# Second router's logits at three places of each feature tile, and the next item's rows transposed inside an earlier product

## The chip, the cores and the metric

The kernel runs on one core of a Trainium2 chip. The metric is the device time of one execution in microseconds (us). The engines are TensorE (PE in the rows; PEld is its loading of weights), VectorE (DVE), ScalarE (ACT), GpSimd (POOL) and SyncE (SP), which issues most transfers.

## The reference

One launch computes an attention layer, a mixture of experts with two experts per token, and a second mixture with one expert per token. The second router can only run on tokens whose first mixture is complete.

```python
def _moe_ref(x, w_gate, w_noise, noise, w1, w2):            # first layer, top 2 of E = 8 experts
    ...
    for e in range(E):
        for k in range(2):
            mask = top2[:, k] == e
            h = np.maximum(x[mask] @ w1[e], 0.0)
            out[mask] += top2_w[mask, k, None] * (h @ w2[e])

def _moe2_ref(x, modality_id, w_gate, modality_bias, w1, w2):   # second layer, one expert per token
    logits = x @ w_gate + modality_bias[modality_id]
    e_idx = np.argmax(logits, axis=1)
    logits_s = logits - logits.max(-1, keepdims=True)
    probs = np.exp(logits_s)
    probs /= probs.sum(-1, keepdims=True) + 1e-09
    gate_w = probs[np.arange(N), e_idx]
    ...
    for e in range(E):
        mask = e_idx == e
        h = np.maximum(x[mask] @ w1[e], 0.0)
        out[mask] = gate_w[mask, None] * (h @ w2[e])

def reference(**kwargs):
    ...
    attn_out = _attn_ref(**attn_kwargs)                     # 4 x 8 heads x 576 x 64
    x = np.ascontiguousarray(attn_out.transpose(0, 2, 1, 3)).reshape(B * S, H * D)
    x = _moe_ref(x=x, **moe_kwargs)                         # N = 2304 tokens, D = 512, F = 1024
    return _moe2_ref(x=x, **moe2_kwargs)
```


## The kernel before

The matrix products of both mixtures are a list of 20 **items**, numbered from 0, each being one expert with a block of gathered token rows. Items 0 to 3 (256 rows) and 4 to 7 (384 rows) are experts 0 to 3 of the first mixture in two parts, items 8 to 11 (640 rows) its experts 4 to 7. Items 12 to 19 belong to the second mixture: item 12 has 512 rows of the expert that the router finds to be the commonest, items 13 and 14 have 256. In the code `L7` is 11, the last item of the first mixture, so `L7 + 1` is item 12.

An item runs over eight **feature tiles**, f = 0 to 7, of 128 hidden features. In the order of issue, f of an item is: loading weights (`_load`) and splitting the weights of two tiles on into a high and a low part (`_split`: `whi` on ScalarE, `wlo` on VectorE or GpSimd); `_first(s + 1)`, which is layer 1 of the next tile (L727, 24 products of 320 columns for 640 rows) with its eviction from PSUM to `hh` (ScalarE, L729) and `hl` (VectorE, L730); then layer 2 of tile f (L739, three products of 512 columns for each block of 128 rows). Item 11 has five such blocks, so 15 products; after the second block `mid()` is called. All engines work through their instructions in the order in which the program issues them.

The `hook` is called three times in each f: with half 0 after layer 1 and ahead of layer 2, with half 2 in `mid()`, and with half 1 after layer 2. The text calls these places **half 0**, **mid** and **end**. In items 11 to 13 the hook runs the second router. `token_tiles` takes two blocks of 128 finished tokens at a place: `px` (L1323) transposes them, at the next place `pl` (L1328) forms their logits, and at the one after `plT` (L1335) transposes the logits back for VectorE (L1337, L1340). There are 18 blocks, so nine places with `px`. Their rows are loaded by SyncE into `x2l`, four blocks at first and two more as two are used up. All these PSUM tiles, and those of layer 1, share one tag, `h`, with three buffers.

Beside this, `back` is a queue of generators that `tick` advances, up to 24 steps per place in item 11. `piece(k)` routes a range of tokens: tops of the logits, then `places` on TensorE (L485 to L488), then the one-hot pairs `ol`, `oh` on VectorE (L526, L527) and `invert` on TensorE (L532). A generator that yields "PE" stops until a later place, and `unblock` lets it go. `choose` finds the commonest expert, `first(item, ...)` finds the rows of item 12: it counts tokens on TensorE (L1380), works out the indices on VectorE (`chd`, L1408, to `pi`, L647), and issues the gather of `xg` on GpSimd (L701). `DONE` names the places at which `need` drives the queue until such a step has been issued.

`_transpose` turns gathered rows into `xh` and `xl`, which layer 1 reads: products `pt` (L710) on TensorE, then ScalarE (L712) and VectorE (L713). For item 12 `tight=1` puts it in f = 7 of item 11, ahead of layer 2, and moves layer 1 of item 12 behind that layer 2.

These few lines of `run` and `second_router` decide the places:

```python
            if nxt and f == nxt.get("at", 0) and i + 1 not in self.rows:
                self._gather(i + 1)
            ...
                n = nxt.get("per", 2)
                j = n * (f - nxt.get("from", FB - 4))
                if nxt and not nxt.get("tight") and j >= 0 and f < FB - 1:
                    self._transpose(i + 1, j, j + n)
```

Of the kernel before, what the change touches and what calls it, by code (L numbers as in the profile page):

```python
# [534 lines left out]
class Items:  # L535
# [87 lines left out]
    def next(self):  # L623

        nc, w, tag, nt = self.nc, self.consts, self.tag, self.nt
        m = w.tile([128, self.most], F32, tag=f"{tag}nm", name="nm")
        j = w.tile([128, self.most], F32, tag=f"{tag}nj", name="nj")
        r = w.tile([128, 1 + nt], F32, tag=f"{tag}nr", name="nr")
        ei = w.tile([128, 1], I32, tag=f"{tag}nei", name="nei")
        nc.vector.tensor_scalar(m, self.ij, self.count, None, op0=ALU.is_equal)  # L630
        for a, src in enumerate([self.ei] + [self.col[:, a] for a in range(nt)]):
            nc.vector.tensor_tensor(j, m, src, op=ALU.mult)
            nc.vector.tensor_reduce(r[:, a:a + 1], j, axis=AX.X, op=ALU.add)
        nc.vector.tensor_copy(ei, r[:, 0:1])
        nc.vector.tensor_scalar(self.count, self.count, 1.0, None, op0=ALU.add)
        return dict(e=ei[0:1], e128=r[:, 0:1], col=[r[:, 1 + a:2 + a] for a in range(nt)])
# [216 lines left out]
def core(ctx, tc, q, k, v, moe_w_gate, moe_w_noise, moe_noise, moe_w1, moe_w2,  # L853
# [37 lines left out]
    ffn = FFN(nc, wpool, DM, F, identF)  # L891
# [4 lines left out]
    with ExitStack() as actx:  # L896
# [135 lines left out]
        back, wait, age = [], [False], [0]  # L1032

        def tick(n=1, pe=False):

            if pe:
                wait[0] = False
            while n and back and not wait[0]:
                n -= 1
                try:  # L1040
                    what = next(back[0])
                    wait[0] = what in ("PE", "PE soon") and not pe
                    age[0] = 2 if what == "PE soon" else 0
                except StopIteration:
                    back.pop(0)

        def unblock(lag=0):

            if wait[0]:
                if age[0] < lag:  # L1050
                    age[0] += 1
                else:
                    wait[0] = False
                    tick(1)
# [147 lines left out]
    def cols(e, j0=0, j1=5):  # L1202
        return [idx[:, e * NT + j:e * NT + j + 1] for j in range(j0, j1)]
# [92 lines left out]
    top = consts.tile([128, 1, E], F32, tag="top", name="top")  # L1296
    tope = consts.tile([128, 1], F32, tag="tope", name="tope")
    topi = consts.tile([128, 1], I32, tag="topi", name="topi")
# [5 lines left out]
    L7 = NX + LAST  # L1304
# [71 lines left out]
    def counts():  # L1376

        yield "PE soon"
        pc = bank2()
        nc.tensor.matmul(pc[:, :E], rt.ones, base2, start=True, stop=True)  # L1380
        yield
        return pc[:, None, :E]

    def need(what):
        while what not in done:
            tick(1, True)

    def choose():

        V = nc.vector  # L1390
        pc = yield from counts()
        cnt, w = (route.tile([128, 1, E], F32, tag=f"ch{n}", name=f"ch{n}") for n in "cw")
        V.tensor_copy(cnt, pc)
        yield
        yield from rt.top(cnt, 1, [top])
        V.tensor_tensor(w, top, rt.iE[:, None], op=ALU.mult)
        yield
        V.tensor_reduce(tope, w, axis=AX.XY, op=ALU.add)
        yield
        V.tensor_copy(topi, tope)  # L1400
        done.add("top")

    def first(item, c0, c1):

        V = nc.vector
        pc = yield from counts()
        d = route.tile([128, 1, E], F32, tag="chd", name="chd")
        V.tensor_scalar(d, pc, -1.0, 128.0 * c1, op0=ALU.mult, op1=ALU.add)  # L1408
        V.scalar_tensor_tensor(topc, tope.to_broadcast([128, 6]), float(NT), rt.iE[:, :6], op0=ALU.mult, op1=ALU.add)
        yield  # L1410
        V.tensor_scalar(d, d, rt.p128, 0.0, op0=ALU.subtract, op1=ALU.max)
        yield
        V.scalar_tensor_tensor(d, d, 128.0, top, op0=ALU.min, op1=ALU.mult)
        yield
        V.tensor_tensor(base2[:, None], base2[:, None], d, op=ALU.add)
        yield from decode2()
        ix = it2.pick(fpool, [topc[:, a:a + 1] for a in range(c0, c1)], ft)
        ffn.items[item].update(rows=lambda: ffn.gather(x2_rows[:, :], ix), out=out2(ix), e=lambda: expert(topi[0:1]),
                               w1=moe2_w1, w2=moe2_w2, ns=128 * (c1 - c0), banks=range(c1 - c0))
        ffn._gather(item)  # L1420
        done.add(item)

    def decode2():
        yield from rt.decode(fs, tab, rt.padh)
        nc.vector.tensor_scalar(ft, fs, rt.pad, None, op0=ALU.subtract)
        yield

    def cut2():
        pc = yield from counts()
        yield from odd_one(pc[:, 0])  # L1430
        yield from it2.cut(pc[:, 0], taken, STATIC)
        done.add("cut")
# [40 lines left out]
    def gates_of(c0, c1):  # L1473
        def write():
            nc.sync.dma_start(x2_rows[128 * c0:128 * c1, DM:DM + 1].rearrange("(t p) c -> p t c", p=128),
                              gate[:, c0:c1, None])
        return write
# [15 lines left out]
    def expert(ap):  # L1493
        return nc.values_load(ap, engines=[mybir.EngineType.SP], min_val=0, max_val=E - 1,
                              skip_runtime_bounds_check_because="experts are counted on the chip")

    def out2(ix):
        def outp(a, p, meta):
            scatter(out, ix[a], weighted(p, meta[:, 0:1])[:, :DM], outs, bounds_check=N - 1, oob_is_err=False)
        return outp  # L1500

    ffn.items[L7 + 1].update(e=lambda: expert(topi[0:1]), at=7, late=True, tight=1)
    ffn.items[L7 + 2].update(e=lambda: expert(topi[0:1]), at=5, **{"from": 5}, pool=True)
    ffn.items[L7 + 3].update(at=1)

# [18 lines left out]
    def load_tiles(n):  # L1524
        for t in loads[:n]:
            x2 = late_pool[0].tile([128, DM], F32, tag="x2l", name="x2l", bufs=4)
            nc.sync.dma_start(x2, x2_rows[128 * t:128 * t + 128, :DM])
            pend.append((t, x2))
        del loads[:n]
# [11 lines left out]
    def token_tiles(n):  # L1541
        new = [(t, x2, wb[:, t, E:]) for t, x2 in pend[:n]]
        del pend[:n]
        tiles(new)
        load_tiles(n)

    def last_tiles(j0, j1):
        tiles([(NT + j, x2, meta[:, E:2 * E]) for j, x2, meta in st2[j0:j1]])

    def piece(k):  # L1550
        c0, c1 = PIECES[k]
        back.append(route2(c0, c1, rt.code[:, c0:c1], gates_of(c0, c1)) if c1 <= NT else
                    route2(c0, c1, code2, gates_last))

    def second_router(i, f, half):

        busy = f == 7 and i == L7
        if half == 0:
            if not busy:
                unblock(1)  # L1560
                tick(TICKS[i - L7])
            return
        h = 2 * (f + 8 * (i - L7)) + half % 2
        if h == 0:
            nc.gpsimd.memset(tab, 0.0)
            fl = fs[:, LAST * NT:LAST * NT + 5]
            rt.encode(code2, fl)
            nc.vector.tensor_scalar(valid[:, NT:], fl, float(N), None, op0=ALU.is_lt)
            nc.vector.tensor_scalar(valid[:, :NT], early, -1.0, 1.0, op0=ALU.mult, op1=ALU.add)
        if h == 1:  # L1570
            load_tiles(4)
        if h == 4:
            rest.extend(ffn.gather(x2_rows[:, :], cols(LAST), tag="rest", bufs=5))
        if h in TILES:
            token_tiles(TILES[h])
        if h in LASTS:
            last_tiles(*LASTS[h])
        if h in WHEN:
            WHEN[h]()
        if not busy:  # L1580
            unblock(1)
            tick(TICKS[i - L7])
        if h in DONE:
            need(DONE[h])

    TICKS = (24, 6, 3)
    DONE = {9: "top", 11: L7 + 1, 25: L7 + 2, 33: "cut"}
    TILES = {**{h: 2 for h in range(2, 11)}, 11: 0, 12: 0}
    LASTS = {17: (0, 2), 18: (2, 4), 19: (4, 5), 20: (5, 5), 21: (5, 5)}

    WHEN = {5: lambda: (piece(0), back.append(choose())), 9: lambda: (piece(1), back.append(first(L7 + 1, 0, 4))),
            12: lambda: (piece(2), back.append(first(L7 + 2, 4, 6))),
            21: lambda: (piece(3), back.append(decode2()), back.append(cut2()))}

    def hook(i, f, half):
        now[0] = i
# [55 lines left out]
```

## Time and profile before

| | us |
|---|---|
| median of 3 runs | 922.13 (921.55 to 924.22) |
| profiled execution | 923.1 |
| its span | 921.4 |
| TensorE busy in the span | 866.3 (94%) |
| VectorE, ScalarE, GpSimd busy | 543.3, 429.3, 322.7 |

The profiled execution is 1.0 us above the median, and 1.7 us of it lie outside its span. A row of a timeline gives the start in us from the span's beginning, the length, engine, line, operation, output and inputs, a count, and in brackets the engine's idle time just before and what ended it. TensorE's products overlap, so a row's length is longer than the step to the next row: a run of products of 512 columns steps by about 0.235 us while each row says 0.39. The clock column is a share of full speed, so 1.00 is 2.4 GHz and 0.50 is 1.2 GHz.

### The profile page before, as it was taken

How to read it: one execution, taken by the hardware profiler on the slowest of the kernel's cores; microseconds unless marked ns; L12 is line 12 of the kernel's file. 1: busy time of each engine (PE TensorE's matmuls, PEld its weight loads, DVE VectorE, ACT ScalarE, POOL GpSimd, SP SyncE). 2: the span in 40 equal slices, each digit the busy share in tenths (PEclk: the TensorE clock that was granted, in tenths of full speed). 3: DMA queues.
4: the chain of work that ended last, by engine and by line, in shares of the span. 5: the costliest groups of instructions: out<-in, count | busy, mean ns of one | idle time of the engine just before them, and what ended most of it. 6: DMA issues, size and time to landing. Idle time of an engine off the chain costs nothing. (4 is left out here: it accounts for less than half of the span.)

```text
span 921.4 us, 18166 instructions
## 1 busy us (share of the span) xinstructions
PE 866.3 (94%) x6775; PEld 760.6 (83%) x6775; DVE 543.3 (59%) x1317; ACT 429.3 (47%) x949; POOL 322.7 (35%) x460
## 2 busy tenths in 40 slices
PE   6998986699999999999999999989989999999995
PEld 5777875598898989999898999978867889999995
DVE  5676796379875544544343443434666877556662
ACT  4575654355554434444233342334423356455662
POOL 7767668235553123043006032050020442222210
PEclk9899998899999999999999999999999999999998
DMA  7868799435886557476328245175423477546660
GB/s 168 179 131 202 175 268 337 151 137 143 275 246 194 147 151 193 142 193 151 126 74 180 92 92 162 46 156 171 129 96 115 149 246 245 186 158 219 209 217 24
DMA packets 158702, 153.83 MB, mean 167 GB/s; under 512 B 74319, under 2 KB 119887, under 8 KB 158608
## 3 DMA queue, kind: packets, MB, share of 16 engines
q1 hardware_dynamic: 143936, 115.43, 41.0%
q0 software_dynamic: 12080, 32.45, 15.2%
q10 hardware_dynamic: 2592, 4.72, 1.4%
q8 instruction: 56, 0.92, 0.4%
q14 instruction: 38, 0.31, 0.1%
HBM read 124.98 MB, written 27.85 MB: 166 GB/s over the span
## 5 line engine op out<-in xcount | busy, mean ns | idle before, releaser
L727 PE MATMUL ph<-xh,whi 128*128 128x256 f32 (+3 forms) x768 | 238.0, 310 | 2.8 <-DVE wlo L688 2.1
L727 PE MATMUL ph<-xl,whi 128*128 128x256 f32 (+3 forms) x768 | 237.1, 309 | 0.4 <-DVE xl L713 0.3
L727 PE MATMUL ph<-xh,wlo 128*128 128x256 f32 (+3 forms) x768 | 237.0, 309 | 0.1
L739 PE MATMUL y<-whi,hh 128*128 128x512 f32 x472 | 191.2, 405 | 0.0
L739 PE MATMUL y<-wlo,hh 128*128 128x512 f32 x472 | 187.2, 397 | 0.0
L688 DVE TENSOR_TENSOR wlo<-raw,whi 128x512 fp32r<-128x512 f32 x135 | 93.3, 691 | 159.2 <-ACT whi L687 147.2
L739 PE MATMUL y<-whi,hl 128*128 128x512 f32 x472 | 186.5, 395 | 0.0
L687 ACT ACTIVATE whi<-raw 128x512 fp32r<-128x512 f32 x160 | 101.0, 631 | 168.4 <-PE y L739 153.8
L727 PEld LDWEIGHTS ph<-xh,whi 128*128 128x128 f32 x768 | 145.6, 190 | 12.7 <-issue 2.6
L727 PEld LDWEIGHTS ph<-xl,whi 128*128 128x128 f32 x768 | 145.6, 190 | 8.3 <-DVE xl L713 1.0
L729 ACT ACTIVATE hh<-ph 128x256 fp32r<-128x256 f32 (+3 forms) x192 | 83.3, 434 | 140.7 <-PE ph L727 133.7
L727 PEld LDWEIGHTS ph<-xh,wlo 128*128 128x128 f32 x768 | 145.8, 190 | 1.8 <-DVE wlo L688 0.3
L730 DVE SCALAR_TENSOR_TENSOR hl<-ph,hh 128x256 fp32r<-128x256 f32 (+3 forms) x192 | 92.5, 482 | 84.1 <-ACT hh L729 81.8
L1196 POOL DMA_INDIRECT x_rows<-y,idx x35 | 57.7, 1648 | 206.6 <-ACT y L1187 106.5
L690 DVE TENSOR_TENSOR wlo<-raw,whi 128x512 fp32r<-128x512 f32 x160 | 119.5, 747 | 12.1 <-ACT whi L689 10.8
L739 PEld LDWEIGHTS y<-whi,hl 128*128 128x128 f32 x472 | 89.0, 188 | 21.2
L739 PEld LDWEIGHTS y<-whi,hh 128*128 128x128 f32 x472 | 89.5, 190 | 13.1 <-DVE y L1189 0.2
L739 PEld LDWEIGHTS y<-wlo,hh 128*128 128x128 f32 x472 | 89.3, 189 | 12.6
L689 ACT ACTIVATE whi<-raw 128x512 fp32r<-128x512 f32 x160 | 98.7, 617 | 0.6 <-DMA raw<-in_moe_w_dram 0.6
L713 DVE TENSOR_TENSOR xl<-pt,xh 128x512 fp32r<-128x512 f32 x59 | 38.8, 688 | 31.0 <-ACT xh L712 30.8
L1196 POOL DMA_INDIRECT out_dram<-y,pi x19 | 20.6, 1084 | 99.6 <-ACT y L1187 44.3
L269 POOL TENSOR_TENSOR Pd<-pe,sm 32x380 f32<-32x380 f32 (+1 forms) x48 | 42.1, 877 | 35.0 <-DVE smd L40 20.0
(302 smaller groups left out, 1076.9 us busy)
## 6 DMA issues: line engine op xcount, KB each, us to landing
raw<-in_moe_w_dram SPq DMA_DIRECT2D x160, 512.0 KB
x_rows<-zero SPq DMA_DIRECT2D x1, 5934.0 KB
vr<-in_v_dram SPq DMA_DIRECT2D x16, 288.0 KB
x_rows<-xr ACTq DMA_DIRECT2D x18, 256.0 KB
x2l<-x_rows SPq DMA_DIRECT2D x18, 256.0 KB
qk<-in_q_dram SPq DMA_DIRECT2D x32, 128.0 KB
qk<-in_k_dram SPq DMA_DIRECT2D x32, 128.0 KB
vw<-in_v_dram SPq DMA_DIRECT2D x24, 128.0 KB
```

What stands on the lines that cost most here:

```text
L269: eng.tensor_tensor(Pd[s, :, W * g:W * g + n], pe[s, :, :n], sm[s, :, None].to_broadcast([W, 2 * NB, n]), op=ALU.mult)
L687: nc.scalar.activation(h1, a, AF.Copy)
L688: eng.tensor_tensor(l1, a, h1.bitcast(F32), op=ALU.subtract)
L689: nc.scalar.activation(hi[:, 1], r2[:, half], AF.Copy)
L690: nc.vector.tensor_tensor(lo[:, 1], r2[:, half], hi[:, 1].bitcast(F32), op=ALU.subtract)
L713: nc.vector.tensor_tensor(xl, p, xh.bitcast(F32), op=ALU.subtract)
L727: nc.tensor.matmul(ps, w[a][:, k], x[b][:, k, s], start=(i == 0), stop=(i == 3 * KD - 1))
L729: nc.scalar.activation(hh[:, s], ps, AF.Relu)
L730: nc.vector.scalar_tensor_tensor(hl[:, s], ps, 0.0, hh[:, s].bitcast(F32), op0=ALU.max, op1=ALU.subtract)
L739: nc.tensor.matmul(p, h[a][:, 128 * j:128 * j + 128], w[b], start=(f == 0 and i == 0), stop=(f == self.FB - 1 and i == 2))
L1196: d = nc.gpsimd.indirect_dma_start(out=dst, out_offset=bass.IndirectOffsetOnAxis(ap=ix, axis=0), in_=y, in_offset=None, **kw)
```

## The change

The hook of item 11 uses half 0 as well as mid and end, so h counts three places for each f there (h = 3f, 3f + 1, 3f + 2) and two for each f from item 12 on (from h = 24). The tables are renumbered. In terms of places: the first `px` moves from f = 1 mid to f = 1 end, and the ninth from f = 5 mid to f = 4 mid; `piece(0)` and `choose` stay at f = 2 end; `piece(1)` and `first` of item 12 move from f = 4 end to f = 4 half 0; the place at which `first` of item 12 must have been issued moves from f = 5 end to f = 6 half 0; `piece(2)` moves from f = 6 mid to f = 6 half 0. Item 12 loses `tight=1` and gets `per=4, from=6`: its four blocks are transposed in f = 6 mid, and its layer 1 is issued ahead of layer 2 of f = 7.

```diff
-    ffn.items[L7 + 1].update(e=lambda: expert(topi[0:1]), at=7, late=True, tight=1)
+    ffn.items[L7 + 1].update(e=lambda: expert(topi[0:1]), at=7, late=True, per=4, **{"from": 6})
...
-        if half == 0:
-            if not busy:
-                unblock(1)
-                tick(TICKS[i - L7])
+        late = i > L7
+        if late and half == 0:
+            unblock(1)
+            tick(TICKS[i - L7])
             return
-        h = 2 * (f + 8 * (i - L7)) + half % 2
+
+        h = 24 + 2 * (f + 8 * (i - L7 - 1)) + half % 2 if late else 3 * f + (0, 2, 1)[half]
...
-        if h == 1:
+        if h == 2:
             load_tiles(4)
...
-    DONE = {9: "top", 11: L7 + 1, 25: L7 + 2, 33: "cut"}
-    TILES = {**{h: 2 for h in range(2, 11)}, 11: 0, 12: 0}
-    LASTS = {17: (0, 2), 18: (2, 4), 19: (4, 5), 20: (5, 5), 21: (5, 5)}
+    DONE = {14: "top", 18: L7 + 1, 33: L7 + 2, 41: "cut"}
+    TILES = {**{h: 2 for h in range(5, 14)}, 14: 0, 15: 0}
+    LASTS = {25: (0, 2), 26: (2, 4), 27: (4, 5), 28: (5, 5), 29: (5, 5)}
...
-    WHEN = {5: lambda: (piece(0), back.append(choose())), 9: lambda: (piece(1), back.append(first(L7 + 1, 0, 4))),
-            12: lambda: (piece(2), back.append(first(L7 + 2, 4, 6))),
-            21: lambda: (piece(3), back.append(decode2()), back.append(cut2()))}
+    WHEN = {8: lambda: (piece(0), back.append(choose())), 12: lambda: (piece(1), back.append(first(L7 + 1, 0, 4))),
+            18: lambda: (piece(2), back.append(first(L7 + 2, 4, 6))),
+            29: lambda: (piece(3), back.append(decode2()), back.append(cut2()))}
```

On TensorE, in f = 5 and 6 of item 11, the count for `first` (L1380) stands in the kernel before behind the last `invert` of f = 5 and ahead of layer 1.

```order
L532 LDWEIGHTS ol
L532 MATMUL rbank<-oh,ol 128x144
L1380 LDWEIGHTS r_ones
L1380 MATMUL rbank<-base_3095,r_ones 128x8
L727 MATMUL ph<-xh,whi 128x320
L727 MATMUL ph<-xl,whi 128x320
```

Behind these rows stand the rest of layer 1's 24 products, six of layer 2 (`y_7576`, `y_7577`), one `plT`, nine more of layer 2, and then the 16 transposes of item 12 (L710). In the changed kernel the count stands behind layer 1, and the transposes follow six products later:

```order
L727 MATMUL ph<-xh,wlo 128x320
L1380 LDWEIGHTS r_ones
L1380 MATMUL rbank<-base_3095,r_ones 128x8
L739 MATMUL y_7576<-whi,hh 128x512
L739 MATMUL y_7576<-wlo,hh 128x512
L739 MATMUL y_7576<-whi,hl 128x512
L739 MATMUL y_7577<-whi,hh 128x512
L739 MATMUL y_7577<-wlo,hh 128x512
L739 MATMUL y_7577<-whi,hl 128x512
L710 MATMUL pt<-gw,xg 128x128 x16
L739 MATMUL y_7578<-whi,hh 128x512
```

So between count and transposes there were 39 products of the item and there are now 6.

On VectorE the same stretch, as a piece of the difference from the last one-hot pair of `piece(1)` to the first instruction behind the count (`chd`):

```order
 L527 TENSOR_SCALAR oh<-r_hHI,lchi,r_code 128x144
-L1337 TENSOR_REDUCE l_3097<-plT 128x16
-L1340 TENSOR_TENSOR l_3097<-l_3097,wb 128x8 x2
 L1373 TENSOR_TENSOR tab<-tab,rbank 128x144
+L688 TENSOR_TENSOR wlo<-raw,whi 128x512
+L690 TENSOR_TENSOR wlo<-raw,whi 128x512
+L730 SCALAR_TENSOR_TENSOR hl<-ph,hh 128x320 x2
 L1408 TENSOR_SCALAR chd<-rbank 128x8
```

The split of a weight tile and both evictions of layer 1 now stand ahead of `chd`, where they stood behind the whole index computation.

On GpSimd the gathers of items 12 and 13 stand in the kernel before as

```order
L701 DMA rest<-x_rows,idx 128x516 x5
L701 DMA xg<-x_rows,pi 128x516 x4
L786 COPY meta<-xg 128x4 x4
L701 DMA xg<-x_rows,pi 128x516 x2
```

and in the changed kernel as

```order
L701 DMA rest<-x_rows,idx 128x516 x5
L701 DMA xg<-x_rows,pi 128x516 x4
L786 COPY meta<-xg 128x4 x4
L701 DMA xg<-x_rows,pi 128x516 x6
```

Four gathers have been added: `_transpose` has dropped item 12's rows at f = 6, so the test of `run` at f = 7 (`at=7`) finds none and gathers the same rows a second time; nothing reads them.

## Rows read from the trace of the kernel before

**Rows 1.** Windows of 20 us: length, then busy PE, PEld, DVE, ACT, POOL; clock, DMA, GB/s.

```profile
620.00:640.00 20.00, 20.00 (x149) 16.22 (x148) 7.67 (x31) 9.22 (x21) 0.60 (x1) 1.00 0.58 201
...
660.00:680.00 20.00, 16.57 (x109) 13.04 (x110) 15.98 (x71) 6.91 (x15) 5.11 (x8) 0.95 0.55 159
```

**Rows 2.** TensorE's own waits from 690 us to the end, one row in all.

```profile
PE pt L710 <- DMA xg<-x_rows,pi: 0.4, 1, 0.4
```

**Rows 3.** Timeline of TensorE in item 11, f = 1 and 2.

```profile
617.02 1.39 PE L1323 MATMUL px<-gw,x2l 128*128 128x128 f32 x8 [2.53 <-DMA x2l<-x_rows]
...
625.62 0.39 PE L739 MATMUL y<-whi,hh 128*128 128x512 f32 x1
...
627.02 0.38 PE L1335 MATMUL plT<-gw,lT 128*128 128x128 f32 x2
627.33 0.64 PE L1328 MATMUL pl<-x2T,g 128*32 128x256 f32 x8
627.90 1.09 PE L1323 MATMUL px<-gw,x2l 128*128 128x128 f32 x8
```

**Rows 4.** Timeline of TensorE in item 11, end of f = 5 to f = 7.

```profile
664.70 0.81 PE L532 MATMUL rbank<-oh,ol 128*128 128x144 f16 x6
665.68 0.22 PE L532 MATMUL rbank<-oh,ol 128*128 128x144 f16 x1 [0.17 <-DVE oh L527]
665.74 0.17 PE L1380 MATMUL rbank<-base,r_ones 128*128 128x8 bf16 x1
...
669.45 0.39 PE L739 MATMUL y<-whi,hh 128*128 128x512 f32 x1
...
672.94 0.40 PE L739 MATMUL y<-whi,hl 128*128 128x512 f32 x1
674.89 0.63 PE L710 MATMUL pt<-gw,xg 128*128 128x128 f32 x4 [1.55 <-DMA xg<-x_rows,pi]
...
677.75 2.04 PE L710 MATMUL pt<-gw,xg 128*128 128x128 f32 x8 [0.80 <-DMA xg<-x_rows,pi]
679.44 0.78 PE L739 MATMUL y<-whi,hh 128*128 128x512 f32 x1
```

**Rows 5.** Timeline of VectorE in item 11.

```profile
626.28 0.49 DVE L730 SCALAR_TENSOR_TENSOR hl<-ph,hh 128x320 fp32r<-128x320 f32 x1 [1.12 <-ACT hh L729]
...
660.03 0.23 DVE L1337 TENSOR_REDUCE l<-plT 128x16 f32<-128x64 f32 x1 [0.66 <-PE plT L1335]
...
661.68 0.17 DVE L498 TENSOR_TENSOR base<-base,more 128x8 bf16<-128x8 bf16 x1 [0.66 <-PE rbank L486]
...
665.30 0.32 DVE L527 TENSOR_SCALAR oh<-r_hHI,lchi,r_code 128x144 f16<-128x144 f16 x1
...
666.16 0.16 DVE L1408 TENSOR_SCALAR chd<-rbank 128x8 f32<-128x8 f32 x1
...
670.06 0.23 DVE L647 TENSOR_SCALAR pi<-ps,r_pad 128x4 int32<-128x4 f32 x1
```

**Rows 6.** Timeline of GpSimd from the gathers of item 12 on.

```profile
671.03 1.27 POOL L701 DMA_INDIRECT xg<-x_rows,pi  x1 [50.43 <-DVE wlo L688]
...
675.12 0.95 POOL L701 DMA_INDIRECT xg<-x_rows,pi  x1 [0.30 <-issue]
...
678.61 0.19 POOL L786 COPY meta<-xg 128x4 f32<-128x4 f32 x1 [0.76 <-DMA xg<-x_rows,pi]
708.94 0.98 POOL L701 DMA_INDIRECT xg<-x_rows,pi  x1 [30.14 <-DVE l L1340]
```

**Rows 7.** Timeline of TensorE at its longest wait, early in the program.

```profile
176.94 1.97 PE L710 MATMUL pt<-gw,xg 128*128 128x128 f32 x8 [5.71 <-DVE lg L969]
```

**Rows 8.** Busy time in windows of 1 us at two places, columns as in rows 1.

```profile
176.00:177.00 1.00, 0.06 (x1) 0.06 (x1) 0.23 (x1) 0.60 (x1) 0.81 (x1) 0.52 0.60 148
...
186.00:187.00 1.00, 1.00 (x6) 0.77 (x5) 0.56 (x2) 0.28 (x2) 0.00 (x0) 0.86 0.00 0
...
681.00:682.00 1.00, 1.00 (x6) 0.80 (x5) 0.94 (x3) 0.00 (x0) 0.00 (x0) 0.89 0.00 0
```

## The prediction

> **What bounds the kernel now.** I read the busy time in windows first. From 620 to 640 us TensorE is busy in 20.00 of 20 us at full clock; from 660 to 680, where item 11 ends, in 16.57, with the clock at 0.95 [rows 1]. Then I asked for TensorE's waits behind that: from 690 us to the end they sum to 0.4 us [rows 2]. So TensorE sets the end from item 11 on, and whatever its queue gains or loses in item 11 arrives at the end unchanged. The timelines of the engines in item 11 then show two places where it stands still. One is the first `px` at f = 1 mid: 2.53 us until the rows `x2l` land [rows 3]. The other is the tight transposition in f = 7: the last product of layer 2 of f = 6 starts at 672.94, layer 2 of f = 7 starts at 679.44, and between them stand 16 transposes with waits of 1.55, some 0.8 and 0.80 us for the gathered rows [rows 4].
>
> **First part: `px` one place later.** The wait ends at 617.02 and began 2.53 earlier, at 614.49 [rows 3]. In the changed kernel the nine products of layer 2 of f = 1 that are left come first. Fifteen such products and a small `plT` run from 669.45 to 673.17 in [rows 4] (672.94 plus a step of 0.23); `plT` costs 0.22 of this with the step back, so fifteen cost 3.5 and nine 2.1. TensorE then asks at 616.6 for rows that land at 617.0: a wait of 0.4 stays, **-2.1 us**. Bounds: -1.5, if the landing that ended the wait was the first block's and the second comes later still, and -2.5, the whole wait.
>
> **Half 0 costs a PSUM wait.** Layer 1 and the router's tiles share three buffers. At half 0, `plT`, `pl` and `px` follow right behind layer 1. The last `hl` that empties a buffer of layer 1 ends at 626.77, 1.15 us after the product that follows layer 1 started [rows 3, 5]; `plT` and `pl` fill only 0.88 of that (627.02 to 627.90 [rows 3]), or 0.57 at f = 2, where there is no `plT`. At mid, six products (1.4 us) cover this wait. There are three such places (f = 2, 3 and 4). Nothing in this trace has the wait, so I bound each from 0 (another buffer is free) to 0.6, and take 0.2, nearer to the 0.3 that the two rows leave than to the upper end: **+0.6 us**, bounds 0 and 1.8.
>
> **`places` of `piece(1)` at f = 5 half 0.** Before, it stood at mid and VectorE was ready ahead of TensorE. Now VectorE must first finish `hl` (to 1.1 us after layer 1). From the logits' reduction at 660.03 to the update of `base` at 661.68 less its wait of 0.66 are 0.99 us, and from there to the end of the last one-hot pair (665.62) 3.94 [rows 5]: in sum 6.0 us after layer 1. TensorE fills `plT` (0.31 [rows 3]), `places` (eight small products, by estimate 0.2, since they overlap as the seven `invert` products do), 15 products (3.5) and seven `invert` products, of which six take from 664.70 to 665.68, less the wait of 0.17, so 0.81, and seven 0.95 [rows 4]: in sum 5.0. It waits about 1.1 where it waited 0.17: **+0.9 us**, bounds 0 and 1.3.
>
> **The transposes at f = 6 mid.** This is the large term. Count from the first product of layer 2 of f = 6. Before, it starts at 669.45, and layer 2 of f = 7 at 679.44: 9.99 us with all of f = 6 and the transposes in them [rows 4]. The count (L1380) stood at 665.74, ahead of layer 1, and covered 3.7 us more of the chain. In the changed kernel the count comes behind layer 1, and `chd` on VectorE behind `hl`, which ends 1.15 after layer 1; with the overlap of one instruction into the next, `chd` starts at 1.1. From `chd` (666.16) to the end of `pi` (670.29) are 4.13 [rows 5]. GpSimd starts the first gather 0.74 later (671.03 [rows 6]). From there to the first product behind the transposes are 8.41 (679.44 [rows 4, 6]). Layer 2 of f = 6 thus resumes 1.1 + 4.13 + 0.74 + 8.41 = 14.4 us after it began, with only six products (1.4) and the transposes done in that time. Nine products more, 2.1, make 16.5 against 9.99, and the `plT` that was inside the 9.99 is paid elsewhere (0.22): **+6.7 us**, bounds 5.9 (`chd` right behind the count) and 7.2 (half a microsecond more in four landings that could vary). No other engine hides any of it: TensorE's own work was the cover, 39 products before and 6 now, and a product behind a waiting one cannot pass it.
>
> Behind the transposes the 2.1 us of layer 2 and `places` still cover `xh` and `xl` of the last block, one instruction each on ScalarE and VectorE, so layer 1 of item 12 need not wait; without that cover it would wait the length of those two. Moving layer 1 of item 12 ahead of layer 2 of f = 7 costs nothing in itself: the same products in another order.
>
> One rule of the Trainium skill bears on the gathers. The last gather's issue ends at 676.07 and its rows are there at 678.61, 2.54 later; the first one's ends at 672.30 and the transposes start at 674.89, 2.59 later [rows 4, 6]. "DMA: Bandwidth & Descriptors", section "Latency and other measured facts", puts the access time of the memory at 0.2 us on average and 2 us under high load, so that a lighter load shortens a transfer's fixed part. By that page the quieter traffic at the new place would give an estimated 1.8 us back, and the sum would be 4.9. By the rows, first and last gather take the same, and I keep 8.41.
>
> **The clock.** After TensorE stood still for 5.71 us until 176.94 [rows 7], the granted clock fell to half (0.52 in the window from 176) and came back within the window from 186, 0.86, that is at 186.3 [rows 8]: 9.3 us after the first transposes. In item 11 now, it came back in the window from 681, 0.89, at 681.2, so 1.8 us of layer 2 ran at half and lost 0.9. In the changed kernel the engine stands idle for 8.4 us ahead of the transposes, so they run at half clock; the first three still wait for landings and lose nothing. If the return takes as long as at 176, it comes 9.3 after the first transposes, 4.7 after resuming, and loses 2.4, 1.5 more than now; if it takes as long as at 674.89 to 681.2, 6.3, it loses no more than now. I take **+0.6 us**, bounds 0 and 1.5.
>
> **Costed at nothing.** The four extra gathers occupy GpSimd for some 5 us (0.95 and a gap of 0.30 each), in a stretch in which it idles for 30.14 us up to item 13's gather at 708.94 [rows 6]; without that cover they would delay item 13's rows by these 5 us. Their 1 MB loads the transfer engines while item 12's third pair of weights is on the way, two feature tiles ahead of its use. The nine pairs of `x2l` are asked for faster, a third of a feature tile apart (a third of 3.7 us of layer 1 and 3.5 of layer 2 [rows 4], and the router's own products) instead of half; the transfers are busy for 0.58 of the time from 620 to 640 [rows 1].
>
> **Sum.** -2.1 + 0.6 + 0.9 + 6.7 + 0.6 = +6.7 us. The profiled execution would go from 923.1 to 929.8; on the median of 922.13 it is **928.8**. The bounds together give +3.4 to +10.3.
>
> **Rivals.**
> - *The gathered rows come in time*, and the kernel ends faster. Then the 3.9 us of waits in the old tight place (6.3 from 673.17 to 679.44 less 2.2 for 16 transposes at full speed) and the clock's 0.9 vanish with the 2.1: -6.9, and with the two small waits +1.5, -5.4: 916.7. For this the chain would have to fit 1.4 us; even to break even it would have to end 6.7 us earlier, at 7.7 after layer 1, and the gathers alone take 8.41. Chance 0.03.
> - *`x2l` is late again.* The wait moves from the first pair to the third or fourth, since transfers for the first pairs, `rest` and a weight pair run together; another 2.5 us as in [rows 3]: 931.3. Against it, pairs two to nine land without a wait today. Chance 0.07.
> - *The second gather of the same rows is in the way*: SyncE's and GpSimd's queues hold weights or item 13's rows behind it, some 3 of its 5 us: 931.8. Chance 0.06.
> - *The gathers land sooner*, because fewer weights are under way beside them than at 671 us: if the last landing took half of its 2.54 us [rows 6], 1.3 less, 927.5. Chance 0.05. The rule of "DMA: Bandwidth & Descriptors" above speaks for this one; the equal landings of first and last gather speak against it.
> - *Nothing measurable* (within 2.8 us, 0.3%, about what these runs can tell): all lower bounds at once, or a chain that starts earlier than the count's row says. Chance 0.03.
> - *The forecast*, with its own range of 925.5 to 932.4: 0.76.
>
> Range for 8 in 10: 925.6 to 932.2, which leaves out the faster case and the ends of the bounds. Faster 0.03, same 0.03, slower 0.94.
>
> **What would show it.** Right: `px` waits at most 0.6 us for `x2l`; a wait of 8 to 9 us ahead of the first L710 of item 12, which stands between the second and third block of layer 2 of f = 6; clock 0.50 from there into layer 2; a wait of about 1 us of the last L532 of f = 5; four further L701 rows on GpSimd in the idle stretch. Wrong: a short wait at L710, which would mean that the chain from the count is shorter than its rows; or a new wait of TensorE in f = 2 to 5 on `x2l` or in item 12 on weights.

## The result: slower by 0.7%, as forecast, and the profile after

The changed kernel takes 928.77 us (median of 7 runs, 925.38 to 932.42) against 921.68 (7 runs, 920.21 to 924.22) beside it: ratio 1.0071, 95% interval 1.0049 to 1.0094, so 4.5 to 8.7 us slower by the interval and 7.1 by the medians. Its profiled execution took 927.92 us, 926.2 of them in the span.

TensorE's waits in the whole changed program, where they answer to [rows 2, 3]: name of the wait, us in total, times, longest.

```profile
PE pt L710 <- DMA xg<-x_rows,pi: 10.4, 5, 7.7
...
PE rbank L532 <- DVE oh L527: 1.4, 6, 0.5
...
PE px L1323 <- DVE hl L730: 0.5, 2, 0.3
...
PE px L1323 <- issue: 0.3, 1, 0.3
```

The 2.53 us ahead of the first `px` have gone and a wait of 7.7 for gathered rows is there. The timeline of TensorE, first at the first `px`, then at one of the two `px` of half 0 that wait for a buffer, then at the end of f = 5:

```profile
613.84 0.66 PE L1323 MATMUL px<-gw,x2l 128*128 128x128 f32 x4 [0.21 <-DMA x2l<-x_rows]
...
632.35 1.09 PE L1323 MATMUL px<-gw,x2l 128*128 128x128 f32 x8 [0.27 <-DVE hl L730]
...
660.52 0.41 PE L532 MATMUL rbank<-oh,ol 128*128 128x144 f16 x2
661.10 0.22 PE L532 MATMUL rbank<-oh,ol 128*128 128x144 f16 x1 [0.17 <-DVE oh L527]
...
662.67 0.22 PE L532 MATMUL rbank<-oh,ol 128*128 128x144 f16 x1 [0.17 <-DVE oh L527]
```

The first `px` waits 0.48 in two pieces (0.21 for the rows and the 0.27 of "issue" above) where it waited 2.53. Five of the seven `invert` products now wait 0.17 each for VectorE. From the first of them to the product behind the last it takes 2.25 us (660.52 to 662.77), where 1.04 did before (664.70 to 665.74 [rows 4]): 1.2 more.

One move is missing from the list of places in "The change": the gather of `rest` kept h = 4, which was f = 2 mid and is f = 1 mid now. It makes no difference here, since GpSimd waits for the rows themselves: the first of these gathers starts 1.60 us after layer 2 of f = 1 begins before (614.53) and 1.54 after (611.50).

The new place of the transposes, on TensorE:

```profile
666.37 0.18 PE L1380 MATMUL rbank<-base,r_ones 128*128 128x8 bf16 x1
666.41 0.47 PE L739 MATMUL y<-whi,hh 128*128 128x512 f32 x1
...
675.77 1.09 PE L710 MATMUL pt<-gw,xg 128*128 128x128 f32 x4 [7.72 <-DMA xg<-x_rows,pi]
677.11 1.09 PE L710 MATMUL pt<-gw,xg 128*128 128x128 f32 x4 [0.25 <-DMA xg<-x_rows,pi]
678.64 1.09 PE L710 MATMUL pt<-gw,xg 128*128 128x128 f32 x4 [0.44 <-DMA xg<-x_rows,pi]
681.26 1.09 PE L710 MATMUL pt<-gw,xg 128*128 128x128 f32 x4 [1.54 <-DMA xg<-x_rows,pi]
682.00 0.78 PE L739 MATMUL y<-whi,hh 128*128 128x512 f32 x1
```

and what this waits for, on VectorE and then on GpSimd:

```profile
667.04 0.49 DVE L730 SCALAR_TENSOR_TENSOR hl<-ph,hh 128x320 fp32r<-128x320 f32 x1 [1.27 <-ACT hh L729]
667.45 0.16 DVE L1408 TENSOR_SCALAR chd<-rbank 128x8 f32<-128x8 f32 x1
...
671.34 0.23 DVE L647 TENSOR_SCALAR pi<-ps,r_pad 128x4 int32<-128x4 f32 x1
```

```profile
672.31 0.95 POOL L701 DMA_INDIRECT xg<-x_rows,pi  x1 [54.74 <-DVE tpk L467]
...
676.07 0.95 POOL L701 DMA_INDIRECT xg<-x_rows,pi  x1 [0.30 <-issue]
...
681.18 0.19 POOL L786 COPY meta<-xg 128x4 f32<-128x4 f32 x1 [2.44 <-DMA xg<-x_rows,pi]
689.44 2.21 POOL L701 DMA_INDIRECT xg<-x_rows,pi  x1 [8.08 <-PE y L739]
```

Layer 2 of f = 6 begins at 666.41, `chd` 1.04 behind it, `pi` ends 4.12 behind that, the first gather starts 0.74 later, and TensorE is back in layer 2 at 682.00, 15.59 us after it began. The row at 689.44 is the first of the four gathers nobody needs. Two windows of 1 us each around the fall and the return of the granted clock (columns as in [rows 1]):

```profile
670.00:671.00 1.00, 0.00 (x0) 0.00 (x0) 0.89 (x7) 0.00 (x0) 0.00 (x0) 0.99 0.00 0
671.00:672.00 1.00, 0.00 (x0) 0.00 (x0) 0.90 (x6) 0.00 (x0) 0.00 (x0) 0.50 0.00 0
...
684.00:685.00 1.00, 1.00 (x5) 0.80 (x4) 0.18 (x2) 0.00 (x0) 0.00 (x0) 0.69 0.00 0
685.00:686.00 1.00, 1.00 (x13) 0.68 (x12) 0.35 (x4) 0.42 (x1) 0.00 (x0) 1.00 0.00 0
```

TensorE stands still from 668.05 (675.77 less 7.72); 2.9 us later the clock is at 0.50, and it is back at 684.6, 2.6 us after layer 2 resumes.

I read the difference in two stretches of TensorE's timeline. From the start of layer 2 of f = 1 (where `px` used to stand) to that of f = 6: 56.45 us (609.96 to 666.41), before 56.52 (612.93 to 669.45). From there to the start of layer 2 of item 12's first tile, called the **bridge** below, which holds the transposes and the end of the chain they wait for: 28.40 (to 694.81), before 20.22 (to 689.67). So all of the loss, 8.2 us in the two profiled executions, is in the bridge. From its end to the start of the last product both take the same (221.6 and 221.8). Their spans differ by only 4.8 us (926.2 and 921.4), because the changed kernel's execution was already 3.0 us ahead in item 10 (its last layer 2 starts at 595.90, before at 598.87), where the programs are the same. So two executions can differ by some microseconds without any change, and a bridge tells the place of a loss better than its size.

### The profile page after: what moved, and what is told of

The parts are those of the page before. It is cut to its first block, busy times and chain, and to the rows that moved or that the text cites. A ratio compares the mean times of both kernels' runs of the same rounds, so it can differ in the third digit from the quotient of the medians.

```text
span 926.2 us, 18177 instructions
## 1 busy us (share of the span) xinstructions
PE 866.9 (94%) x6775; PEld 760.0 (82%) x6775; DVE 544.8 (59%) x1317; ACT 429.6 (46%) x949; POOL 325.8 (35%) x464
```

## The experiments

The bridge is that of the one profiled execution; the ratio is that of 12 runs (7 of the changed kernel, 6 of the run that gathers once) to those of the kernel before on the same chip. Rows are to be compared by these ratios; their medians come from more than one chip and from different times. "Resumes" counts from the first product of layer 2 of f = 6 to the first product of layer 2 behind the transposes.

| what differs | median us | ratio (95%) | resumes after | bridge |
|---|---|---|---|---|
| before | 921.7 to 922.9 | 1 | 9.99 | 20.22 |
| after | 928.77 | 1.0071 (1.0049 to 1.0094) | 15.59 | 28.40 |
| rows gathered once | 930.55 | 1.0080 (1.0053 to 1.0107) | 15.90 | 29.60 |
| router's places alone | 926.78 | 1.0049 (1.0031 to 1.0067) | 14.32 | 25.26 |
| transposes' place alone | 923.32 | 1.0012 (0.9991 to 1.0033) | 10.88 | 24.17 |
| after, count at f = 5 end | 923.83 | 1.0012 (0.9994 to 1.0030) | 10.22 | 22.18 |
| after, 20 fillers | 927.14 | 1.0047 (1.0025 to 1.0068) | 14.21 | 27.18 |
| after, 72 fillers | 926.37 | 1.0043 (1.0024 to 1.0062) | 13.96 | 25.57 |
| router's places, count at f = 5 end | 923.47 | 1.0001 (0.9979 to 1.0023) | 12.17 | 22.52 |
| the same, `piece(2)` at f = 6 mid | 922.11 | 0.9992 (0.9977 to 1.0008) | 10.39 | 21.59 |
| the same, `piece(1)` at f = 4 end | 923.08 | 0.9999 (0.9982 to 1.0017) | 10.37 | 21.35 |
| the same, transposes at f = 7 mid | 920.06 | 0.9974 (0.9958 to 0.9989) | 9.99 | 18.01 |
| before, transposes behind f = 7 | 922.33 | 1.0000 (0.9974 to 1.0026) | | 21.16 |
| router's places, count at f = 5 end, transposes behind f = 7 | 925.86 | 1.0024 (0.9999 to 1.0049) | | 24.60 |

**Are the four extra gathers in the way?** In the changed kernel:

```diff
-... at=7, late=True, per=4, **{"from": 6})
+... at=9, late=True, per=4, **{"from": 6})
```

> The changed kernel without the second gather of item 12's rows (at=9). Theory (four more gathers in an idle stretch cost nothing): the time of the changed kernel, 7.1 us above before, within 1. Rival (they hold back weights or item 13's rows): 3 to 5 us less than the changed kernel, so 2 to 4 above before. If they cause the changed kernel's wider spread (925.4 to 932.4, where before has 920.2 to 924.2), the spread narrows to 4 us.

930.55 us, 0.8% above before. Without them the kernel is no faster, so the rival is out, and the wider spread of the runs is not theirs either: 926.9 to 932.2 without them, and the kernel before, too, spread from 919.0 to 926.2 in more runs.

**Which of the two moves costs what?** First the new places with the old transposes (`tight=1` put back in the changed kernel), then the other way round, the kernel before with item 12's line of the change (the second gather comes with it).

```diff
-... late=True, per=4, **{"from": 6})
+... late=True, tight=1)
```

> The changed router places alone: the transposes of item 12 stay in f = 7 (tight=1), the count for its rows stands at f = 6 half 0. Theory (the count behind layer 1 sets when the rows are there): layer 2 of f = 7 starts 14.4 us (the prediction's chain) to 15.6 us (the changed kernel's trace) after layer 2 of f = 6 began, where it was 9.99; -2.1 for px, +0.5 and +1.2 for the two small waits, -0.2 for plT, +4.4 to +5.6, clock up to +0.5: 3.8 to 5.5 us slower than the kernel before. Rival (the transposes' new place is the whole loss, and the router's new places only gain): the time is that of before less 2.1 plus 1.7, at most 0.5 us faster.

```diff
-... late=True, tight=1)
+... late=True, per=4, **{"from": 6})
```

> The transposes in f = 6 mid alone, the router at its old places (the count ahead of layer 1 of f = 7). Theory: the rows are there as in the kernel before, about 10 us after layer 2 of f = 6 began, and only the nine products that no longer cover the wait are lost, 2.1, less 0.2 for plT, and up to 1 for the clock: 2 to 3 us slower than before. Rival (the place of the transposes is the loss, wherever the count stands): the changed kernel's +7.1, plus the 2.1 of px that is not gained, less 1.7 for the small waits: 7 to 8 us slower.

The places alone cost 0.49%, 4.5 us (2.9 to 6.2), as the theory has it, and `tight=1` does not save them: layer 2 of f = 7 starts 14.32 after that of f = 6, and the chain of the prediction says 14.4. The transposes' place alone costs 0.12% (-0.1 to 0.3%, so -0.8 to 3.0 us): the 2 to 3 us that were expected are neither shown nor excluded. Its bridge is 3.95 longer, of which 2.1 are the nine products of lost cover, 0.9 the later return to layer 2, and 0.9 the clock (the nine products took 3.95 there). But this profiled execution took 925.99, 2.7 above the median of its run, with the lowest mean clock of the twelve (0.969; their median is 0.976). The rival with 7 to 8 us is out.

**The count moved back alone**, in the kernel that gathers once:

```diff
-    DONE = {14: "top", 18: L7 + 1, ...
+    DONE = {14: "top", 17: L7 + 1, ...
```

> The changed kernel, rows gathered once, with the count for item 12's rows driven to f = 5 end, ahead of layer 1 of f = 7; the transposes stay in f = 6 mid. Theory (the count's place is the larger half of the loss): rows about 10 us after layer 2 of f = 6 began; -2.1 + 0.5 + 1.2 + 2.1 - 0.2 + 0.5 to 1 for the clock: 2.0 to 2.5 us slower than before, 4.5 to 5 below the changed kernel. Rival (the place of the transposes alone): the changed kernel's +7.

One number in a table takes back 6.7 us of the 7.9 by the medians. TensorE's first wait at L710 shrinks from 7.73 to 3.94. So the count's place carries most of the loss. What is left for the transposes' place, with the count ahead of layer 1, is 1.1 us with an interval of -0.6 to 2.8, not to be told from nothing.

**Why did the fourth block wait 1.5 us?** In the changed kernel the last gather's issue ends at 677.02 and its rows are there at 681.18, 4.16 later (before: 2.54), and 4.47 when gathered once; the runs with either move alone show 2.7 and 3.0. The transfer queues of the changed kernel from 678.5 to 679.4, then from 679.4 to 680.7 (packets, MB, share of 16 engines):

```profile
q0 software_dynamic: 50, 0.14, 43.1%
q8 instruction: 1, 0.02, 7.9%
...
q0 software_dynamic: 4, 0.01, 4.7%
```

q0 carries the gather. Besides, one packet of 16 KB with instructions runs from 678.59 for 1.14 us. All of the gather but four packets is done by 679.32; these four (three of 4128 bytes and the closing one) start at 679.72, 680.15, 680.50 and 680.68, one after the other, the first as the instruction packet ends. By these times, one transfer engine had the instruction packet ahead of its share of the gather; the trace does not name a packet's engine. The run that gathers once shows the same: the instruction packet from 680.94 to 681.89, and the last four packets of the gather from 681.88 on. In the runs with either move alone, whose last gather was not late, it runs ahead of the gathers (at 668.75, places alone) or behind the last landing (at 680.48, transposes' place alone, landing at 678.30). To move that packet I put 20 transposes of a constant on TensorE where it stands idle:

```diff
+                if self.items[i].get("tight") is None and self.items[i].get("late") and self.items[i].get("per") == 4:
+                    p = self.psum.tile([128, self.KD, 128], F32, tag="h", name="pfill", bufs=3)
+                    for n in range(20):
+                        self.nc.tensor.transpose(p[:, n % 4], self.identF, self.identF)
             for j in range(j0, min(j1, ns // 128)):
```

> The changed kernel with 20 transposes of a constant, whose result nobody reads, put on TensorE right ahead of item 12's transposes, where it stands idle for 7.7 us: they cost nothing and let the instruction packet that TensorE's progress calls for be fetched some 40 instructions earlier. Theory (that packet of 16 KB holds up three packets of the last gather on one transfer engine for 1.4 us): it lands ahead of the gathers, the fourth wait at L710 falls from 1.5 to 0.4 us, and the time is 1.2 to 1.6 us below the changed kernel's, 5.5 to 6 above before. Rival (the fourth gather is late for reasons of its own): the wait stays at 1.5 to 1.9 and the time at +7.

```profile
666.87 0.18 PE L1384 MATMUL rbank<-base,r_ones 128*128 128x8 bf16 x1
...
677.69 1.09 PE L710 MATMUL pt<-gw,xg 128*128 128x128 f32 x4 [0.34 <-DMA xg<-x_rows,pi]
679.17 2.29 PE L710 MATMUL pt<-gw,xg 128*128 128x128 f32 x8 [0.39 <-DMA xg<-x_rows,pi]
...
681.11 0.78 PE L739 MATMUL y<-whi,hh 128*128 128x512 f32 x1
```

The fourth block follows without a wait (x8 in one row), TensorE resumes 14.21 after layer 2 of f = 6 began (666.90), and the packet runs at 666.42, ahead of the gathers. The ratio is 0.24% below the changed kernel's (1.6 us by the medians) and 0.33% below that of the run that gathers once, but the intervals overlap: that the wait goes with the packet is shown in the traces, that the time falls is not. How the packet's time is set I can't say.

**What does the clock cost?** The same with `range(72)`:

> As the run with 20 filling transposes, with 72 of them, which at 0.106 us each (eight took 0.85) fill the idle time ahead of item 12's transposes up to some 0.5 us. Theory (the idle time halves the granted clock, and that is a loss of its own): the clock stays up, the last block's transposes and the nine products behind them run at full speed, TensorE resumes 13.3 instead of 14.2 us after layer 2 of f = 6 began and then saves 1.2: 2 us below the run with 20, 2.5 to 3 above before. Rival (the clock falls all the same in the waits between the four blocks, as it does in the kernel before): the time of the run with 20, +4.8.

```profile
676.00:677.00 1.00, 1.00 (x11) 1.00 (x10) 0.28 (x2) 0.25 (x1) 0.69 (x2) 1.00 0.00 0
...
682.00:683.00 1.00, 0.46 (x4) 0.22 (x2) 0.37 (x1) 0.51 (x1) 0.00 (x0) 1.00 0.27 107
```

The fillers are the busy column of the first window; the clock stays at 1.00 through the waits of 0.75 to 0.81 between the blocks. The nine products behind the transposes take 2.19 us (683.59 to 685.78); at the falling clock they took 3.38 in the changed kernel. The bridge is 1.6 shorter than with 20 fillers, where 2 were expected, since resuming gains only 0.25 (13.96 for 14.21) instead of 0.9. The time shows no difference (1.0043 and 1.0047), so the clock's price is read from the trace alone: 1.2 us on these nine products.

**A version without the loss.** The router's new places with the count at f = 5 end and `tight=1`:

```diff
-... late=True, per=4, **{"from": 6})
+... late=True, tight=1)
...
-    DONE = {14: "top", 18: L7 + 1, ...
+    DONE = {14: "top", 17: L7 + 1, ...
```

> The router's new places with the transposes in f = 7 as before and the count for item 12's rows driven to f = 5 end, ahead of layer 1 of f = 7, as before. Theory: -2.1 for px, +0.5 and +1.2 for the two small waits and nothing else: 0.4 us faster, not to be told from no change. Rival (the router's new places cost in themselves): as slow as the run with the changed places alone, +4.1.

No difference from before within 2 us, so the new places cost nothing that these runs can tell as long as the count stays ahead of layer 1, and the rival's 4.1 is out. In the traces, too, they neither gain nor cost: from layer 2 of f = 1 to that of f = 6 the changed kernel and the ten runs with the new places take 56.45 to 56.99 us, and the kernel before and the two runs with the old ones 56.51 to 56.54. But the bridge is 2.3 longer, with a wait that the kernel before doesn't have. TensorE, and then VectorE ahead of it:

```profile
679.02 1.11 PE L710 MATMUL pt<-gw,xg 128*128 128x128 f32 x4 [1.95 <-DVE xl L713]
```

```profile
676.86 0.30 DVE L527 TENSOR_SCALAR oh<-r_hHI,lchi,r_code 128x144 f16<-128x144 f16 x1
677.09 0.68 DVE L688 TENSOR_TENSOR wlo<-raw,whi 128x512 fp32r<-128x512 f32 x1
677.69 0.68 DVE L690 TENSOR_TENSOR wlo<-raw,whi 128x512 fp32r<-128x512 f32 x1
678.29 1.87 DVE L713 TENSOR_TENSOR xl<-pt,xh 128x512 fp32r<-128x512 f32 x3
```

The first `xl` starts at 678.29, though its transposes stood at 672.94: the one-hot pairs of `piece(2)`, which has moved from f = 6 mid to half 0, are ahead of it. The fourth block finds all three buffers taken. So `piece(2)` goes back, and then `piece(1)` too:

```diff
-            18: lambda: (piece(2), ...
+            19: lambda: (piece(2), ...
```

> The run with the new places, the count at f = 5 end and tight=1, with piece(2) put back from f = 6 half 0 to f = 6 mid. Theory (piece(2)'s VectorE work stands ahead of xl, so that the fourth block's transposes wait 1.95 us for a PSUM buffer): that wait goes, layer 2 of item 12 starts 20.2 us after that of f = 6, as before, instead of 22.5: 2 us less than that run, and the kernel before within 0.5. Rival (the wait for xl comes from the transposes' own order): no change from that run.

```diff
-    WHEN = {8: ..., 12: lambda: (piece(1), ...
+    WHEN = {8: ..., 14: lambda: (piece(1), ...
```

> px at its new places and all routing work at its old ones (piece(1) at f = 4 end, piece(2) at f = 6 mid, the count at f = 5 end, tight=1). Theory: -2.05 for x2l, +0.27 and +0.5 for the waits of px, and the L532 waits of 0.8 and their 0.4 of lost overlap gone: 1.3 us faster than before, at the edge of what can be told. Rival (px at half 0 costs more than it gains): no change or slower.

The first takes the wait for `xl` away and the bridge from 22.52 to 21.59 (the ratios, 0.9992 and 1.0001, can't be told apart), but not down to 20.2: the clock is back only at 681.7, 3.9 us after TensorE resumes (677.82), where it took 1.8 before. The second was a miss: the five L532 waits of 0.17 stay, 0.8 in sum, so they do not come from the place at which `piece(1)` begins, and 1.3 us were not gained. The rows show where they come from. VectorE needs 3.94 us from the update of `base` to its last one-hot pair in the kernel before (661.68 to 665.62 [rows 5]) and in this run (660.70 to 664.64). In the kernel before, TensorE had these router products between layer 2 and the first `invert`:

```profile
663.82 0.38 PE L1335 MATMUL plT<-gw,lT 128*128 128x128 f32 x2
664.12 0.64 PE L1328 MATMUL pl<-x2T,g 128*32 128x256 f32 x8
```

These 0.88 us (663.82 to 664.70) now stand elsewhere, and TensorE waits about as long instead, product by product. So the wait follows from the new places of `px` themselves, wherever `piece(1)` begins. Then the transposes into the middle of layer 2 of f = 7:

```diff
-... late=True, tight=1)
+... late=True, tight=3)
             def mid():
...
+                if tight == 3:
+                    self._transpose(i + 1)
```

> The run before this one with item 12's transposes in the middle of layer 2 of f = 7 instead of ahead of it. Theory (TensorE's own products are the only cover of the rows): six products, 1.4 us, come ahead of the waits of 3.9 and the nine behind them cover xh and xl: 1.4 below the run before this one, 2.5 to 3 us faster than the kernel before. Rival (the last landing, or a buffer that VectorE holds, ends last wherever the transposes stand): no gain beside the run before this one.

```profile
669.61 0.39 PE L739 MATMUL y<-whi,hh 128*128 128x512 f32 x1
...
675.02 0.63 PE L710 MATMUL pt<-gw,xg 128*128 128x128 f32 x4 [0.34 <-DMA xg<-x_rows,pi]
676.39 0.66 PE L710 MATMUL pt<-gw,xg 128*128 128x128 f32 x4 [0.74 <-DMA xg<-x_rows,pi]
677.96 0.63 PE L710 MATMUL pt<-gw,xg 128*128 128x128 f32 x4 [0.92 <-DMA xg<-x_rows,pi]
679.22 0.63 PE L710 MATMUL pt<-gw,xg 128*128 128x128 f32 x4 [0.63 <-DMA xg<-x_rows,pi]
679.60 0.48 PE L739 MATMUL y<-whi,hh 128*128 128x512 f32 x1
```

0.9974 (0.9958 to 0.9989): 1 to 4 us faster than the kernel before, and faster than both kernels of this case. TensorE resumes 9.99 after layer 2 of f = 6 began, exactly as before, but with six products more behind it, and the clock stays at 1.00 throughout. Hence the 2.2 of the bridge: 1.4 of cover, and the 0.9 that the clock took before. By the times, the gain over the run before this one is less certain than that over the kernel before, since their intervals (0.9958 to 0.9989 and 0.9982 to 1.0017) just overlap. Why the clock stayed up is open. The first wait is 0.34 where it was 1.55, but in the run with the new places, the count at f = 5 end and `tight=1` it was 0.64, followed by 0.77 and 0.97, and the clock fell there ahead of the third block's transposes at 675.98:

```profile
675.00:676.00 1.00, 0.03 (x2) 0.05 (x1) 1.00 (x6) 0.60 (x1) 0.10 (x1) 0.74 0.84 219
```

**Even later: behind layer 2 of f = 7**, with the kernel before (`tight=1` made `tight=2`) and with the new places:

> The kernel before with item 12's transposes put behind layer 2 of f = 7 (tight=2). Theory (the chain of the rows ends about 9.4 us after layer 2 of f = 6 began, wherever TensorE asks): the 15 products of layer 2 of f = 7, 3.5 us, cover the waits of 3.9, and xh and xl of the last block, some 1.5, come into the open: 2 to 3 us faster. Rival (the evictions of item 11's five blocks stand ahead of xh and xl on VectorE and ScalarE): 3 us more in the open, no change or up to 1 us slower.

> The router's new places with the count ahead of layer 1 of f = 7 and the transposes behind layer 2 of f = 7. Theory: the sum of the two parts, -0.4 and -2 to -3: 2.5 to 3.5 us faster than before. Rival (evictions ahead of xh and xl): 0.5 us slower to 0.5 faster.

Twelve transposes then run without any wait, but the fourth block waits 2.1 us for a buffer, and with the new places 5.1:

```profile
674.63 3.38 DVE L1487 SCALAR_TENSOR_TENSOR x<-y,meta,rest 128x512 f32<-128x512 f32 x5
677.92 1.87 DVE L713 TENSOR_TENSOR xl<-pt,xh 128x512 fp32r<-128x512 f32 x3
```

These are VectorE's rows of the first of the two: the evictions of item 11's five blocks (L1487) stand ahead of `xl`. The rival's mechanism was right in both. The first came out at no gain, as it said. The second came out at +0.24%, 2.2 us (-0.1 to 4.5), where it said at most 0.5: `piece(2)` stands at half 0 in it, its one-hot pairs (to 676.55) are ahead of the same evictions, and these begin 10.6 us after layer 2 of f = 6 where they begin 7.0 after it in the first.

## Why the prediction was right, point by point

**`px` one place later**, -2.1: 2.53 fell to 0.48, 2.05 gained. **Half 0's PSUM wait**, +0.6: 0.5, at two of the three places. **`places` of `piece(1)`**, +0.9: mis-sized; 1.2, since five of the products wait for VectorE one by one instead of the last one alone. Its reason, half 0 and the `hl` ahead of VectorE, is only one way to this wait: with `piece(1)` back at its old place the five waits stay, because `plT` and `pl` no longer stand ahead of `invert`. The sum of the three is -0.35, and with the 0.2 of the `plT` that is paid here -0.1; the stretch up to f = 6 shortened by 0.07, so up to there the change gains nothing.

**The transposes at f = 6 mid**, +6.7: the mechanism held link by link. The prediction's chain is 1.1 + 4.13 + 0.74 + 8.41; measured are 1.04, 4.12, 0.74 and 9.69. The last link was mis-sized by 1.3, and that is the fourth landing, behind the instruction packet. The wait ahead of the first block was 7.72 where 8 to 9 were named, since the first gather's issue took 0.95 instead of 1.27 [rows 6]. With the packet elsewhere the chain takes 14.21, and 14.32 with the places alone, both beside the 14.4 of the prediction. With the 15.59 and nine products more, the term comes to 7.9 instead of 6.7. The runs with one half of the change show that most of it comes from the count, which lost the 3.7 us of layer 1 and stands behind `hl`; the nine products of lost cover, 2.1, stand in the traces, and the times leave them open.

**The clock**, +0.6: nine products took 3.38 instead of 2.1, 1.3 lost where 0.9 were lost before, so +0.4, inside its bounds.

**Costed at nothing:** the extra gathers are, as the run without them shows; TensorE's waits from 690 us on are 0.4 again. The rivals: `x2l` late again has no row (0.21 at the first `px`, none later). In the rival of rows that come in time, 6.3 less 2.2 is 4.1 and not 3.9, which moves only that rival's time, by 0.2. The gathers landing sooner: the first one's issue ends at 673.26 and the transposes start at 675.77, 2.51 against 2.59 before. By the Trainium skill, "DMA: Bandwidth & Descriptors", section "Latency and other measured facts", a lighter load on the memory makes a transfer's fixed part smaller. No run here tests that, since the load was not lighter: between the end of the first issue and the first transposes only packets of the gathers ran in either kernel, 98 before (131 GB/s) and 99 now (137 GB/s). So the premise of this rival, fewer weights beside the gathers, did not hold, and the last landing was later, not earlier.

In the profiled executions the two stretches give -0.07 + 8.2 = +8.1, and the terms as measured (-2.05, 0.5, 1.2, 7.9 and 0.4) 8.0; forecast were +6.7, and the medians differ by 7.1. So the mechanism was right, but that 6.7 comes so close to 7.1 is in part luck: the forecast knew nothing of the instruction packet, which alone is 1.3, and the interval of 4.5 to 8.7 holds 6.7 and 8.1 alike. What stays open: most bridges differ from that of before by some 1 to 3 us more than the times of the same kernels do (the transposes' place alone: 3.95 longer in the bridge, 1.1 by the ratio). Each bridge is of one execution, and these took up to 2.7 us more and up to 1.2 us less than the median of their run. Nearly all the differences have the same sign, so the 20.22 of the one execution of the kernel before may be short for that kernel; that is not shown.

## What to carry to other kernels

Where an engine waits for data that it ordered itself (here a count, indices, a gather, rows), look at the place where the chain starts and the place where it is needed together: one number in a table that moved the count behind 3.7 us of TensorE's work cost 6.7 us by the medians, more than the whole wait of 2.53 that the change removed. Put the wait where the waiting engine's products can cover it and where the engine that empties its buffers has nothing else queued: in the traces here the middle of the last layer 2 (bridge 18.01) was better than ahead of it (21.35, waits in the open), and better than behind it in the kernel before (21.16, evictions on VectorE). And two places that trade a wait of 2.5 us for several of 0.2 to 0.3 can come out even.

## What the hardware showed that I had not expected

An instruction packet of 16 KB took 1.14 us on the transfer queues, and a gather beside it was held up, by the times of the packets on the transfer engine that the two shared: the last rows came 4.16 and 4.47 us after the issue's end in the two runs in which it fell between the last gather's issue and its landing, and 2.5 to 3.0 in the others.

The clock fell to 0.50 in the kernel before at waits of 1.55, 0.81 and 0.80 and in another run at 0.64, 0.77 and 0.97, and stayed at 1.00 in the best version at 0.34, 0.74, 0.92 and 0.63, and with 72 fillers ahead of waits of 0.79, 0.81 and 0.75. It came back 1.8 us after TensorE resumed in the kernel before, 2.6 in the changed kernel and 3.9 in the run with `piece(2)` put back, so its price is not one number, not even for waits as alike as those of the first and the last of these.
